# Where in an expert's group the zero rows for a later group are sent: behind the results of the group ahead, or in the middle of the group

## The chip, the cores and the metric

The kernel runs on one core of a Trainium2 chip. The metric is the device time of one execution in microseconds, the median of several runs. A core has TensorE (PE, matrix products), VectorE (DVE), ScalarE (ACT), GpSimd (POOL) and SyncE (SP); SP and POOL issue nearly all of the transfers here, SP by hardware queues and POOL by one software queue. A line such as L842 is line 842 of the kernel.

## The reference

Attention over 4 batches, 8 heads, 768 positions and 64 columns a head, with a mask that keeps the first `n_global` keys and the last `n_local`, and a bias by distance. Its output, 3072 tokens of 512 values, goes through a layer of 8 experts; each token uses only the expert with the highest gate.

```python
logits = x @ w_gate
expert_idx = np.argmax(logits, axis=1)
...
for e in range(E):
    mask = expert_idx == e
    ...
    xe = x[mask]
    h = np.maximum(xe @ w1[e], 0.0)
    ye = h @ w2[e]
    out[mask] = gate_w[mask, None] * ye
```

Here `w1[e]` is 512 x 1024 and `w2[e]` 1024 x 512, all in 32-bit floats.

## The kernel before

**Stages.** The first 160 us or so are attention, 24 blocks of 128 positions. Each block's tokens are sent by an indirect transfer (`scatter`, L627) to a table in HBM, `xg_dram`, which has one region of rows for each expert. Then come the groups, in the order 0, 8 (a small one, for late tokens of expert 0), 1, 2, ..., 7: one expert at a time, up to 512 token rows. With some 3072 / 8 = 384 tokens to an expert, the rows of a region behind the last token would hold whatever lay in HBM before, so rows of zeros are written there.

**The zeros.** For groups 0, 1 and 8 all 512 (or 128) rows are cleared beforehand by SP (`blank`). For groups 2 to 7, `pads(g)` issues four indirect transfers from POOL (L755), one for each 128 rows of the region, with the table `pad` of row numbers: a row that holds a token gets a number beyond the table, and the transfer leaves it out. The source is `zeros`, 128 rows of 516 words in SBUF.

**A group.** `group(p)` computes the up product (512 to 1024), ReLU, and the down product (1024 to 512). Both use a scheme with seven block products in place of eight (`seven`): the up product is made in two halves `j` of seven steps, the down product in one, so that a group has steps 0 to 13 and D = 14 to 20. A step of the up product is eight matmuls, one of the down product sixteen. The products are called one, two, three, four, five, six and last, in this order of issue. In each, TensorE writes a PSUM bank (L842), and a reader takes it: ScalarE copies product one (L870), VectorE takes two (L874), ScalarE three (L879, with ReLU, into the tile `h`; L881 in the down product), VectorE four (L885), five (L901), six (L906) and last (L911), each of the last three followed by a ReLU on ScalarE (L866). Product three adds to the bank of product one, so it waits for L870's copy. In the first half of groups 1 to 7, the columns beyond 208 of the first four products are made in a separate part ahead of product five, `rest` (L889 to L897). L879 of the second half (step 9) writes `h[:, 2:4, 0]`.

VectorE also makes the sums that the scheme needs: of the weights (`w_sums`, L710 to L713), of the tokens (`x_sums`, L812 to L815) and of the hidden values (`h_sums`, L925 to L928), and turns the tokens (`x_in`, L806).

**Order of the other work.** Engines run the instructions in the order in which the program records them. `at_(i, ...)` hangs work behind step i. In group p, with `nxt` the next group and `after` the one behind that:

- at the start SP loads the next group's tokens and gates, which wait for that group's zeros: `ex.load_x(nxt, [f"pad{nxt}.{j}" for j in range(4)])` (L779 and L788);
- in steps 0 and 1 the results of the group ahead are turned back (L821), scaled with the gate (L824) and sent to the output by four indirect transfers from POOL (`send`, L832);
- behind step 4 POOL issues `pads(after)`. Nothing on POOL lies between the sends and these;
- behind D and D + 6 SP loads the weights of `after` (L690, L693).

`pads(2)` is issued ahead of these, in group 0, by `all_counts`; groups 1 to 5 issue `pads(3)` to `pads(7)`.

**Waits.** The program records what each operation reads and writes (`_r` and `_w` add to it) and derives from that which semaphores it waits for. A transfer's reads and writes count until it has landed.

Of the kernel before, what the change touches and what calls it, by code (L numbers as in the profile page):

```python
# [634 lines left out]
class Experts:  # L635
# [113 lines left out]
            out=self.xs[g * self.REGION:g * self.REGION + 128 * n, :].rearrange("(j p) w -> p j w", p=128),  # L749
            in_=self.zero.bitcast(I32).unsqueeze(1).to_broadcast([128, n, self.XW]), _w=[f"pad{g}"], _r=[self.zero])  # L750

    def pads(self, g):

        for j in range(4):
            self.f.pool.indirect_dma_start(  # L755
                out=self.xs[:], out_offset=bass.IndirectOffsetOnAxis(ap=self.keep["pad"][:, g, j:j + 1], axis=0),
                in_=self.zeros.bitcast(I32), in_offset=None, bounds_check=self.xs.shape[0] - 1, oob_is_err=False,
                _r=[self.keep["pad"][:, g, j:j + 1], self.zeros], _w=[f"pad{g}.{j}"])

    def pad_table(self, g0, g1):  # L760
        k, V = self.keep, self.f.dve
# [214 lines left out]
def kernel(  # L976
# [60 lines left out]
    with ExitStack() as stack:  # L1037
# [6 lines left out]
        f = Flow(tc)  # L1044
# [3 lines left out]
        ex = Experts(f, dict(moe_w1=moe_w1, moe_w2=moe_w2, xs=xg_dram, XW=XW, REGION=NTOK, out=out), psum, keep,  # L1048
                     (Arena(big, 0, WSET), Arena(big, WSET, WSET)), Arena(big, 2 * WSET, 22560 - 2 * DM), small[:, 0:XW], ylast[:])
# [26 lines left out]
        def sums_part(n):  # L1076

            us = at.sums(n - 2, U)
            at.tokens_x(n - 2, T0)
            us()  # L1080
            at.tokens_u(n - 2, U)
# [109 lines left out]
        def all_counts():  # L1191
            V.tensor_tensor(keep["cnt"][:, 1:E], base_e[:, 1:E], keep["gbase"][:, 1:E], ALU.subtract)
            ex.tables(1, E)
            ex.pad_table(2, E)
            f.pool.memset(ex.zeros, 0.0)
            ex.pads(2)

        order = [0, E, *range(1, E)]
        forms = [(keep["index"][0:1, g:g + 1], ex.SIZES, f"form{g}") for g in range(E)]
# [39 lines left out]
        def group(p):  # L1239

            g = order[p]
            nxt = order[p + 1] if p + 1 < len(order) else None
            after = order[p + 2] if p + 2 < len(order) else None
            todo = {}

            def at_(i, *fns):
                todo.setdefault(i, []).extend(fns)

            def run(steps, first):
                for i, fn in enumerate(steps, first):  # L1250
                    fn()
                    for fn in todo.pop(i, ()):
                        fn()
# [35 lines left out]
            if g == 0:  # L1289

                run(ups[:1], 0)
                sums_part(N + 1)
                run(ups[1:2], 1)
                pieces = ex.w_pieces(1)

                def scatters():
                    for u in range(NBLK):
                        at.scatter(B - 1, u)
                    last = sum(tokens, [])
                    ex.load_x(E, last)  # L1300
                    for fn in pieces[:4]:
                        fn()
                    ex.load_x(1, last)

                at_(2, lambda: at.normal(N - 1, U), lambda: at.choose(B - 1), *pieces[4:])
                at_(4, lambda: at.counts(U), lambda: at.gates(B - 1))
                at_(5, lambda: at.slots(B - 1, U))
                at_(6, lambda: at.rows(N - 1, T0), scatters)
                at_(9, late_counts)
                at_(D, all_counts)  # L1310
                at_(D + 3, lambda: ex.marks(E))
                at_(D + 4, lambda: ex.x_in(E, 0))
            elif g == E:
                sums, pieces, xs = ex.w_sums(1, True), ex.w_pieces(2), ex.x_sums()
                at_(0, sums[0], sums[1])
                at_(1, sums[2], check_sums)
                at_(2, check)
                at_(3, lambda: f.hint(*forms[1]), lambda: ex.x_in(1, 0), lambda: ex.x_in(1, 1), xs[0], xs[1])
                at_(4, xs[2], xs[3], lambda: ex.marks(1), *pieces[:4])
                at_(5, *pieces[4:])  # L1320
            else:
                if nxt is not None:
                    sums, xs = ex.w_sums(nxt, True), ex.x_sums()
                    at_(13, lambda: ex.x_in(nxt, 0))
                    at_(D + 1, lambda: ex.x_in(nxt, 1), sums[0])
                    at_(D + 3, xs[0], xs[1])
                    at_(D + 4, sums[1])
                    at_(D + 5, sums[2])
                    at_(D + 6, xs[2], xs[3], lambda: ex.marks(nxt))
                if after is not None:  # L1330
                    pieces = ex.w_pieces(after)
                    at_(4, lambda: ex.pads(after))
                    at_(D, *pieces[:4])
                    at_(D + 6, *pieces[4:])

# [9 lines left out]
        for p in range(len(order)):  # L1345
            group(p)
# [429 lines left out]
```

## Time and profile before

| | us |
|---|---|
| median of 3 runs | 517.89 (516.78 to 520.77) |
| the profiled execution's own time | 517.95 |
| its span, first to last instruction | 516.1 |
| TensorE busy | 478.7 |
| VectorE busy | 352.5 |
| ScalarE busy | 174.1 |
| GpSimd busy | 166.0 |

The profile is of one execution. A row of the table by stage has the stretch in us from the start, its length, then for PE, PEld (weight loads), DVE, ACT and POOL the busy time and the number of instructions, then TensorE's granted clock, the mean busy share of the 16 DMA engines, and GB/s. A row of the waits has who waited, for whom, the sum in us, how often, and the longest. A row of the timeline has start and length in us, engine, line, operation, what it writes and reads, and in brackets how long the engine was idle before and what ended that. An end of a matmul is modelled, and some matmul records can be missing. A transfer of POOL is shown for the time in which POOL works on it.

### The profile page before, as it was taken

What the parts mean: (1) busy time and instruction counts of PE and PEld (TensorE: products, weight loads), DVE (VectorE), ACT (ScalarE), POOL (GpSimd) and SP (SyncE); (2) the same over time, 40 slices, a digit from 0 to 9 for tenths busy, and PEclk for the clock granted to TensorE, in tenths of its full rate; (3) what the DMA queues carried; (4) which work ended last, traced back from release to release, by engine and by line L of the source; (5) the groups of instructions that cost most, each with busy time, mean ns of one, the idle gap of its engine ahead of it and who ended that gap; (6) DMA issues with size and microseconds to landing.
All of it is one profiled execution on the core that took longest, in us unless ns stands there. A gap on an engine that the chain in (4) does not pass through costs nothing. (4 is left out here: it accounts for less than half of the span.)

```text
span 516.1 us, 10775 instructions
## 1 busy us (share of the span) xinstructions
PE 478.7 (93%) x4397; PEld 451.3 (87%) x4397; DVE 352.5 (68%) x626; ACT 174.1 (34%) x306; POOL 166.0 (32%) x192
## 2 busy tenths in 40 slices
PE   3999999999977999999998999997999999999980
PEld 3888888888866899999998999997999999999980
DVE  4654775897873884666775885865877667687840
ACT  3766555555543230323122223212204203303410
POOL 1554465667664053330024016006006103003011
PEclk9999999999997999999999999999999999999996
DMA  9999999998424437897783774656368378001000
GB/s 152 205 242 244 183 238 245 241 224 187 103 99 110 161 127 165 210 244 175 162 222 116 159 211 117 144 186 164 75 176 219 101 181 228 7 1 48 18 25 29
DMA packets 120344, 79.24 MB, mean 154 GB/s; under 512 B 86422, under 2 KB 103318, under 8 KB 120272
## 3 DMA queue, kind: packets, MB, share of 16 engines
q1 hardware_dynamic: 112960, 63.77, 55.9%
q0 software_dynamic: 6480, 14.45, 8.0%
q8 instruction: 51, 0.84, 0.7%
q14 instruction: 21, 0.17, 0.1%
q10 hardware_dynamic: 832, 0.02, 0.1%
HBM read 61.39 MB, written 23.71 MB: 165 GB/s over the span
## 5 line engine op out<-in xcount | busy, mean ns | idle before, releaser
L842 PE MATMUL psum<-arena 128*128 128x208 f32 (+5 forms) x1776 | 293.4, 325 | 8.1 <-ACT arena L870 6.5
L842 PEld LDWEIGHTS psum<-arena 128*128 128x128 f32 x1776 | 285.1, 190 | 12.6 <-ACT arena L870 8.0
L832 POOL DMA_INDIRECT out_dram<-arena,to x16 | 21.8, 1365 | 218.5 <-ACT arena L824 193.8
L501 DVE TENSOR_TENSOR arena<-psum,arena 128x1024 f32<-128x1024 f32 x40 | 48.8, 1219 | 37.2 <-PE psum L491 37.2
L515 POOL TENSOR_TENSOR arena<-arena 128x512 f32<-128x512 f32 x40 | 53.4, 1334 | 35.9 <-ACT arena L509 35.9
L509 ACT ACTIVATE arena<-arena 128x1024 f32<-128x1024 f32 (+1 forms) x48 | 47.4, 987 | 47.7 <-DVE arena L501 36.1
L491 PE MATMUL psum<-arena 64*128 64x128 f32 x704 | 50.2, 291 | 1.2 <-ACT arena L477 0.7
L866 ACT ACTIVATE arena<-arena 128x512 f32<-128x512 f32 x48 | 30.2, 630 | 61.2 <-DVE arena L901 30.8
L491 PEld LDWEIGHTS psum<-arena 64*128 64x128 f32 x704 | 45.0, 197 | 5.9 <-issue 3.4
L528 PE MATMUL psum<-arena 128*64 128x128 f32 x704 | 43.9, 277 | 0.2 <-issue 0.2
L870 ACT COPY arena<-psum 128x512 f32<-128x512 f32 (+1 forms) x24 | 13.5, 561 | 84.8 <-PE psum L842 83.2
L528 PEld LDWEIGHTS psum<-arena 128*64 128x64 f32 x704 | 38.2, 137 | 3.3 <-issue 0.6
L627 POOL DMA_INDIRECT xg_dram<-arena,slot_i x24 | 24.7, 1030 | 23.3 <-DVE arena L911 15.8
L911 DVE TENSOR_TENSOR arena<-arena,psum 128x512 f32<-128x512 f32 x24 | 16.5, 689 | 21.9 <-PE psum L842 18.3
L885 DVE TENSOR_TENSOR arena<-arena,psum 128x512 f32<-128x512 f32 (+1 forms) x24 | 15.8, 659 | 22.0 <-PE psum L842 20.7
L755 POOL DMA_INDIRECT xg_dram<-small,pad x24 | 25.7, 1070 | 12.5 <-issue 7.0
L906 DVE TENSOR_TENSOR arena<-arena,psum 128x512 f32<-128x512 f32 x24 | 16.5, 688 | 15.9 <-PE psum L842 14.2
L901 DVE TENSOR_TENSOR arena<-arena,psum 128x512 f32<-128x512 f32 x24 | 16.5, 688 | 14.8 <-PE psum L842 13.6
L467 PE MATMUL psum<-ident,arena 128*128 128x128 f32 x96 | 16.1, 294 | 8.7 <-DMA arena<-in_k_dram 7.1
L832 POOL DMA_INDIRECT out_dram<-ylast,to x17 | 17.4, 1025 | 20.6 <-ACT ylast L824 12.7
L874 DVE TENSOR_TENSOR arena<-arena,psum 128x512 f32<-128x512 f32 (+1 forms) x24 | 15.8, 656 | 11.0 <-PE psum L842 9.8
L713 DVE TENSOR_TENSOR arena<-arena 128x1024 f32<-128x1024 f32 x16 | 19.9, 1243 | 3.0 <-issue 2.9
(152 smaller groups left out, 535.2 us busy)
## 6 DMA issues: line engine op xcount, KB each, us to landing
arena<-in_moe_w_dram SPq DMA_DIRECT2D x64, 512.0 KB
arena<-xg_dram SPq DMA_DIRECT2D x64, 128.0 KB
arena<-in_q_dram SPq DMA_DIRECT2D x24, 256.0 KB
arena<-in_k_dram SPq DMA_DIRECT2D x24, 256.0 KB
arena<-in_v_dram SPq DMA_DIRECT2D x24, 256.0 KB
xg_dram<-arena SPq DMA_DIRECT2D x2, 1032.0 KB
xg_dram<-arena,slot_i POOLq DMA_INDIRECT x24
xg_dram<-small,pad POOLq DMA_INDIRECT x24
```

What stands on the lines that cost most here:

```text
L491: f.pe.matmul(self.psum[:, 2 * g + a, c:c + P], lhsT=kt[r, m, :], rhs=qt[r, m, :], start=True, stop=True, skip_group_check=True)
L501: f.dve.tensor_tensor(e, s, self.bias[:, g, :, 1:3, :].rearrange("p h k c -> p h (k c)"), ALU.add)
L509: f.act.activation(e, e, AF.Exp)
L515: f.pool.tensor_tensor(self.es[n % 3][:, g], e[:, :, 0:P], e[:, :, P:2 * P], ALU.add)
L528: f.pe.matmul(po[r, m, :], lhsT=self.v[(n - ab) % 6][:, 2 * m + a, :], rhs=self.e[n % 2][:, m // 2, 2 * a + m % 2, P * ab:P * ab + P], sta ...
L627: self.f.pool.indirect_dma_start(out=self.xs[:], out_offset=bass.IndirectOffsetOnAxis(ap=k["slot_i"][:, b % 2, u:u + 1], axis=0), in_=self ...
L713: lambda: V.tensor_tensor(c["t4"], c["b21"], c["t2"], ALU.subtract)]
L755: self.f.pool.indirect_dma_start(out=self.xs[:], out_offset=bass.IndirectOffsetOnAxis(ap=self.keep["pad"][:, g, j:j + 1], axis=0), in_=sel ...
L832: return pool.indirect_dma_start(out=self.out[:], out_offset=bass.IndirectOffsetOnAxis(ap=self.keep["to"][:, g, j:j + 1], axis=0), in_=sel ...
L842: f.pe.matmul(self.psum[:, bank, 256 * t + cut.start:256 * t + cut.stop], lhsT=w[k][:, ts(t, 128)], rhs=x[k][:, cut], start=(fresh and t = ...
L866: f.act.activation(d, d, act)
L901: V.tensor_tensor(dst["c22"], u3, bank(W), ALU.add)
```

## The change

`pads` gets a second argument, `behind`, which each of its four transfers is declared to read: nothing is taken from it, but the transfers wait until it has been written, and a later write to it waits until they have landed. In groups 1 to 5 the call moves from behind step 4 to behind step 10, with `h[:, 2:4, 0]` as that argument, which L879 writes in step 9. `pads(2)` stays where it is and names `zeros`, which it reads anyway. The same transfers are issued, in the same order on every engine.

```diff
-    def pads(self, g):
+    def pads(self, g, behind):
...
-                _r=[self.keep["pad"][:, g, j:j + 1], self.zeros], _w=[f"pad{g}.{j}"])
+                _r=[self.keep["pad"][:, g, j:j + 1], self.zeros, behind], _w=[f"pad{g}.{j}"])
...
-            ex.pads(2)
+            ex.pads(2, ex.zeros)
...
-                    at_(4, lambda: ex.pads(after))
+                    at_(10, lambda: ex.pads(after, ex.h[:, 2:4, 0]))
```

## The prediction

> **What bounds the kernel now**
>
> I read the page first, then the busy times by stage, TensorE's waits in the expert stage, and last the timeline around each run of GpSimd's transfers.
>
> ```profile
> PE 478.7 (93%) x4397; PEld 451.3 (87%) x4397; DVE 352.5 (68%) x626; ACT 174.1 (34%) x306; POOL 166.0 (32%) x192
> L755 POOL DMA_INDIRECT xg_dram<-small,pad x24 | 25.7, 1070 | 12.5 <-issue 7.0
> ```
>
> TensorE is the bound. GpSimd is idle for two thirds of the span, so time saved or lost on it counts only through what it disturbs. The stage table covers groups 1 to 6, one row each: length, then TensorE's busy time.
>
> ```profile
> 226.00:265.00 39.00, 39.00 (x224) 38.97 (x223) 26.48 (x37) 7.57 (x14) 5.13 (x5) 1.00 0.77 188
> 265.00:305.00 40.00, 37.72 (x243) 37.35 (x242) 29.84 (x43) 10.07 (x18) 8.43 (x8) 1.00 0.64 163
> 305.00:346.00 41.00, 40.44 (x243) 39.75 (x242) 29.68 (x42) 10.11 (x19) 10.25 (x8) 1.00 0.59 153
> 346.00:388.00 42.00, 38.47 (x247) 37.62 (x246) 30.00 (x43) 10.44 (x20) 8.75 (x8) 1.00 0.61 156
> 388.00:430.00 42.00, 41.81 (x244) 41.11 (x242) 29.75 (x43) 10.23 (x20) 10.18 (x8) 1.00 0.62 159
> 430.00:470.00 40.00, 39.56 (x235) 38.86 (x234) 28.73 (x40) 9.39 (x17) 4.85 (x4) 1.00 0.25 64
> ```
>
> TensorE loses 7.0 us here in all, nearly all in two groups. The clock column is 1.00 throughout, so no throttle is behind it. The waits from 225 to 470 us name what ended the idle time:
>
> ```profile
> PE psum L842 <- ACT arena L870: 6.5, 4, 3.5
> PE psum L842 <- DVE arena L901: 0.4, 1, 0.4
> ```
>
> All four waits for L870 (ScalarE's copy of product one) fall at the same step, the start of the second half of the up product: 2.28 us at 279.6, 0.52 at 318.2, 3.51 at 362.1 and 0.19 at 400.7. The worst, in the timeline:
>
> ```profile
> 352.81 5.79 PE L842 MATMUL psum<-arena 128*128 128x184 f32 x35
> ...
> 354.03 0.97 POOL L755 DMA_INDIRECT xg_dram<-small,pad  x1 [0.30 <-issue]
> ...
> 356.64 0.69 DVE L906 TENSOR_TENSOR arena<-arena,psum 128x512 f32<-128x512 f32 x1 [2.11 <-PE psum L842]
> ...
> 357.87 0.97 POOL L755 DMA_INDIRECT xg_dram<-small,pad  x1 [0.30 <-issue]
> 360.22 0.69 DVE L911 TENSOR_TENSOR arena<-arena,psum 128x512 f32<-128x512 f32 x1 [2.89 <-remote]
> ...
> 361.48 0.57 ACT L870 COPY arena<-psum 128x512 f32<-128x512 f32 x1
> ...
> 362.10 25.04 PEld L842 LDWEIGHTS psum<-arena 128*128 128x128 f32 x160 [3.79 <-ACT arena L870]
> 362.10 25.36 PE L842 MATMUL psum<-arena 128*128 128x184 f32 x160 [3.51 <-ACT arena L870]
> ```
>
> TensorE's records run on without a gap to 358.6, eight matmuls in 1.25 us, but the engines that take its results get them late: L906 comes 2.80 us after L901, L911 3.58 us after L906. So TensorE had computed and its signals were late; then it stops, because product three may not start before L870 has copied product one. GpSimd is meanwhile in the second half of an unbroken row of eight indirect transfers, four sends (L832) and four of zeros (L755), from 347.96 to 358.84.
>
> I then set each such row against TensorE's idle time. Rows of eight (from 267.2, 307.0, 348.0, 389.5): 2.28, 0.52, 3.51, 0.19 us. Five (one send, four of zeros, 227.3 to 233.7): none. Four sends alone (from 208.8, 431.3, 472.2): 0, 0.43, 0. Four of zeros alone (196.8 to 201.6): none. Six scatters from 182.9: none; but six from 147.6 end with the 2.7 us wait of L553. Signals are late from about 6 us after the row's start. Two rows without loss:
>
> ```profile
> 193.81 12.99 PE L842 MATMUL psum<-arena 128*128 128x176 f32 x86
> ...
> 438.70 7.54 PE L842 MATMUL psum<-arena 128*128 128x200 f32 x43 [0.43 <-DVE arena L901]
> ```
>
> The first spans the four transfers of zeros by themselves with TensorE never idle; the second shows the dearest row of sends alone.
>
> **What the Trainium skill says**
>
> "Perfetto Trace Analysis", section "Tensor Engine Instruction (MATMUL, LD_WEIGHTS)": a matmul's end in the profile is estimated, and the semaphore moves only after PSUM has acknowledged the writes. So unbroken matmul records beside late readers are possible, as seen here; why the signal comes late it doesn't say.
>
> The same page, "DMA Instruction — SWDGE (GPSIMD)": the interval shown ends when descriptors are written, not when data moves. The trace agrees: the last one of zeros ends at 358.84, and GpSimd's queue moves packets until after 360.
>
> "SBUF — State Buffer", section "Who interferes with whom": a VectorE operation with two SBUF inputs contends with GpSimd instructions that read SBUF, and the first one holds the port. Here one side pays: a transfer beside L712 takes 2.02 instead of 0.97 us, while L712 itself takes 1.22 to 1.28 us.
>
> "DMA: Bandwidth & Descriptors", section "SWDGE vs HWDGE vs iDMA": GpSimd's transfers have one queue, and the engines take turns between it and the hardware queues. So zeros today stand behind the sends in one queue. The page gives nothing on signals of TensorE.
>
> **The change part by part**
>
> Counts: no instruction goes. Five groups (1 to 5) issue pads four times each, so 20 transfers of 0.97 us, 1.28 us from start to start, move from step 4 to step 10. The first additionally waits for L879 of the second half. pads(2) keeps its place; its extra argument adds nothing.
>
> 1. *The row of eight is cut.* In the group from 305 the zeros now run from 313.5 to 319.4; L879 ends at 320.5, so they would run from about 320.6 to 325.4 (3 x 1.28 + 0.97), some 7 us behind the last send. The stalls of the four rows of eight go: -6.5 us. What is left is four rows of sends alone: by the three seen, 0.43 us in three, 0.14 each, so +0.6 us (0 to 1.7). Group 1 has only one send before its zeros and loses nothing today.
>
> 2. *The zeros in the new place.* They lie beside products four to seven of the second half and the start of the down product. Nearest row: the four alone at 196.8, no stall. But the place is tighter: in the group from 430 product five ends near 436.9 by TensorE's records and L901 starts at 437.95, a signal some 1.0 us late that cost 0.43 us, so it had about 0.5 us to spare; and the down product's second product needs L926, which ends at 327.6, about 0.4 us before TensorE comes to it. I take 0, and keep 0.5 us for each of five groups (2.5 us) as the upper end. Below zero it can't go: TensorE has no gap there to win.
>
> 3. *VectorE.* Beside the zeros it has L925 to L928, nine sums with two SBUF inputs, instead of L712. At most 0.06 us each (1.28 against 1.22), 0.5 us a group, inside the same 0.4 to 0.5 us of room, and inside the upper end above. Taken as 0.
>
> 4. *The added waits.* GpSimd's wait holds only the other three pads; behind them come the next group's sends, some 20 us later. L879 now also waits for the four transfers of the group before, since they count as readers of that tile; these landed over 30 us earlier, and L879 stands idle 1.6 us for TensorE today. 0, at most 0.2 us on ScalarE, which is 34% busy.
>
> 5. *Who reads the zeros, and the other queues.* load_x of the next group waits for them in SP's queue, at 345.3 for the zeros that would land near 328: 17 us of room. The weight loads at 325.6 may share the engines with 0.26 MB of zeros for about 1.5 us at the 179 to 229 GB/s seen there; those weights are read one group later. 0.
>
> Sum: -6.5 + 0.6 = -5.9 us on the profiled execution's 517.95 us: 512.05, say 512.1. Its own time lies 0.06 us from the median 517.89, so nothing is added. Ends: 511.4 (no residue) and 511.4 + 1.7 + 2.5 = 515.6.
>
> **The rivals**
>
> *The lateness goes along with the zeros* (B). For it: late signals lie beside the zeros rather than the sends in all four rows, and in the row from 348 they go on after other transfers have ended. Against it: zeros alone at 196.8 and one send with zeros at 227.3 cost nothing. Then about 6 us come back in the new place: 517.9, between 515.6 and 519.
>
> *It was never the row* (C). The small loads of gates (8 bytes each) and the instruction fetch near 354.3 fall in the same microseconds, and stay. For it: the group from 430 has such loads and a fetch, no zeros, and a late signal; against it: that cost 0.43 us, not 3.5. 517.9.
>
> *Slower* (D). Zeros are late on their own and strike where there is only 0.4 to 0.5 us of room, in five groups instead of four. Priced by the two worst stalls, mean 2.9 us, with 0.4 us less room: 3.3 x 5 - 5.9 = +10.6 us, 528.5. It decides against the change from 1.2 us of new idle time a group (5.9 / 5), and over 1% from 2.2 us. Against it: again the row at 196.8.
>
> **How the numbers follow**
>
> The likeliest case 0.66, B 0.16, C 0.07, D 0.11. A measurement of this kernel tells about 1% from no change (5.2 us). The likeliest case passes that if the residue stays below 1.3 us, three times in four: faster 0.50. Within 1%: 0.16 of it and B and C, 0.39. Slower: D, 0.11. The likeliest case by itself spans 511.4 to 515.6; the range reaches a little below it for the scatter of the runs (516.78 to 520.77) and up to 518.2 to take in most of B and C; D is left out.
>
> **What would show it**
>
> Right: TensorE's waits for L870 fall from 6.5 us to under 1.5; L901, L906 and L911 follow each other at one product's length (1.25 to 1.41 us) again; GpSimd's rows in groups 2 to 5 break into four and four, with L755 about 0.1 us behind L879. Wrong: waits for L901, L874 or L885 of the down product in their place (B, D), or L870 still waited for beside rows of four (C).

## The result, and the profile after

The kernel after takes 509.94 us (509.14 to 512.12, 5 runs) against 517.89 us (516.26 to 520.77): ratio 0.986, 95% interval 0.9824 to 0.9896, faster by 1.4%. The forecast, 512.1 us, had the direction and the mechanism; the gain was 7.95 us where 5.9 was worked out, and the time lies 1.1 us below the range. The profiled execution after is the fastest of its five (509.14 us).

The page after, engines and the group of the zeros:

```profile
PE 476.9 (94%) x4397; PEld 452.2 (89%) x4397; DVE 352.8 (70%) x626; ACT 174.0 (34%) x306; POOL 163.4 (32%) x192
L755 POOL DMA_INDIRECT xg_dram<-small,pad x24 | 23.4, 974 | 52.5 <-ACT arena L879 41.5
```

The same 24 transfers, now behind a wait for L879 (41.5 us of idle time on GpSimd) and each a little shorter, 974 ns in place of 1070: in the kernel before, three of them that began while L711 or L712 was running had taken 1.23, 2.02 and 1.94 us, and none begins there now. Next the table by stage, cut at the first L870 of each group so that each row is one whole group, 1 to 6:

```profile
225.12:264.95 39.83, 39.83 (x230) 39.79 (x229) 26.64 (x37) 8.24 (x16) 4.88 (x5) 1.00 0.77 189
264.95:302.24 37.29, 37.29 (x242) 37.21 (x241) 29.61 (x42) 9.96 (x18) 8.42 (x8) 1.00 0.65 173
302.24:342.10 39.86, 39.86 (x242) 39.79 (x241) 29.64 (x42) 10.09 (x18) 9.20 (x8) 1.00 0.62 157
342.10:379.69 37.59, 37.57 (x242) 37.18 (x241) 29.62 (x42) 9.97 (x19) 8.75 (x8) 1.00 0.66 170
379.69:420.82 41.13, 41.13 (x242) 41.06 (x241) 29.62 (x42) 10.07 (x18) 9.20 (x8) 1.00 0.67 160
420.82:460.97 40.15, 40.13 (x242) 39.74 (x241) 29.63 (x42) 10.09 (x19) 4.84 (x4) 1.00 0.28 71
sum 235.85, PE 235.82 PEld 234.78 DVE 174.75 ACT 58.42 POOL 45.29; mean PE 39.30 PEld 39.13 DVE 29.13 ACT 9.74 POOL 7.55
```

TensorE is busy for 235.82 of 235.85 us. The same cut of the kernel before, its groups 2 and 4, which had lost most, and the sum of all six:

```profile
265.17:305.01 39.84, 37.56 (x242) 37.19 (x241) 29.68 (x42) 10.07 (x18) 8.43 (x8) 1.00 0.64 163
345.97:387.50 41.53, 38.00 (x242) 37.15 (x241) 29.53 (x42) 9.97 (x19) 8.75 (x8) 1.00 0.60 154
sum 244.84, PE 237.84 PEld 234.50 DVE 174.67 ACT 58.47 POOL 47.60; mean PE 39.64 PEld 39.08 DVE 29.11 ACT 9.75 POOL 7.93
```

The span fell by 8.8 us (516.1 to 507.3): 8.99 in these six groups and 0.22 ahead of group 1, while 0.41 came back behind group 6. By group, 1 to 6, the fall is 0, 2.55, 1.10, 3.94, 0.72 and 0.68 us. The weight loads' time is the same to 0.3 us: no work went, only idle time. TensorE's waits from 225 to 470 us by its weight loads, in the kernel before:

```profile
PEld psum L842 <- ACT arena L870: 7.7, 4, 3.8
PEld psum L842 <- DVE arena L874: 1.3, 4, 0.3
PEld psum L842 <- DVE arena L901: 0.7, 1, 0.7
```

and what is left of them after:

```profile
PEld psum L842 <- DVE arena L874: 0.7, 2, 0.3
PEld psum L842 <- DVE arena L901: 0.2, 1, 0.2
```

No wait for L870 remains. In the timeline, the group that had lost most:

```profile
347.81 10.49 PE L842 MATMUL psum<-arena 128*128 128x208 f32 x66
...
349.68 0.69 DVE L901 TENSOR_TENSOR arena<-arena,psum 128x512 f32<-128x512 f32 x1 [0.19 <-issue]
...
350.85 0.69 DVE L906 TENSOR_TENSOR arena<-arena,psum 128x512 f32<-128x512 f32 x1 [0.49 <-PE psum L842]
...
352.10 0.69 DVE L911 TENSOR_TENSOR arena<-arena,psum 128x512 f32<-128x512 f32 x1 [0.56 <-PE psum L842]
...
353.36 0.57 ACT L870 COPY arena<-psum 128x512 f32<-128x512 f32 x1
...
357.31 0.97 POOL L755 DMA_INDIRECT xg_dram<-small,pad  x1 [7.45 <-ACT arena L879]
```

L901, L906, L911 and L870 follow each other every 1.17 to 1.26 us, one product's length, where they had been 2.80, 3.58 and 1.26 us apart; GpSimd rests 7.45 us between the last send and the first zeros.

The traces also hold the times at which each engine's semaphore was raised, the signal that the readers wait for. In group 4 of the kernel before, three products end by TensorE's records at 356.10, 357.35 and 358.59 us; matched in order (a few are missing from the trace), their signals come at 360.20, 360.29 and 360.38 us, so 4.10, 2.94 and 1.79 us late, where half of all of TensorE's signals follow within 0.02 us. Three products that take 1.25 us each were not computed in 0.18 us, so it was the signals that were late and not the work. No signal of VectorE, ScalarE or GpSimd is over 0.02 us late in that trace. In the kernel after, none of TensorE's that the trace holds is over 0.3 us late in groups 1 to 6.

### The profile page after: what moved, and what is told of

Read it like the earlier page. It is cut to its first block, busy times and chain, and to the rows that moved or that the text cites. A ratio compares the mean times of both kernels' runs of the same rounds, so it can differ in the third digit from the quotient of the medians.

```text
span 507.3 us, 10785 instructions
## 1 busy us (share of the span) xinstructions
PE 476.9 (94%) x4397; PEld 452.2 (89%) x4397; DVE 352.8 (70%) x626; ACT 174.0 (34%) x306; POOL 163.4 (32%) x192
## 5 line engine op out<-in xcount | busy, mean ns | idle before, releaser
L870 ACT COPY arena<-psum 128x512 f32<-128x512 f32 (+1 forms) x24 | 13.5, 561 | 81.8 <-PE psum L842 81.6
L755 POOL DMA_INDIRECT xg_dram<-small,pad x24 | 23.4, 974 | 52.5 <-ACT arena L879 41.5
L911 DVE TENSOR_TENSOR arena<-arena,psum 128x512 f32<-128x512 f32 x24 | 16.5, 688 | 17.7 <-PE psum L842 17.2
L906 DVE TENSOR_TENSOR arena<-arena,psum 128x512 f32<-128x512 f32 x24 | 16.5, 688 | 14.7 <-PE psum L842 13.4
L901 DVE TENSOR_TENSOR arena<-arena,psum 128x512 f32<-128x512 f32 x24 | 16.5, 688 | 12.8 <-PE psum L842 11.5
L874 DVE TENSOR_TENSOR arena<-arena,psum 128x512 f32<-128x512 f32 (+1 forms) x24 | 15.8, 657 | 8.5 <-PE psum L842 8.1
```

The lines of the kernel that those rows point to most:

```text
L755: self.f.pool.indirect_dma_start(out=self.xs[:], out_offset=bass.IndirectOffsetOnAxis(ap=self.keep["pad"][:, g, j:j + 1], axis=0), in_=sel ...
L901: V.tensor_tensor(dst["c22"], u3, bank(W), ALU.add)
```

## The experiments

Each kernel was timed beside the kernel before on the same chip, on three chips in all. The kernel before took 513.11 us beside four of them (the place without the wait, all rows written, gates loaded later, eight zeros in the middle), 514.29 us beside the next four (the kernel after once more, the first split, the short pause, the row of six cut at the end of attention) and 518.03 us beside the last four (the second split, rows of nine and twelve, the late place, memsets). Ratios with their intervals are therefore what is compared, and the length of each group in the profiled execution, cut as above. The table gives how much longer each group was than in the kernel after (differences of -0.01 are given as 0.00). Each row is one execution; the kernel before was profiled only in the first measurement, on another chip than these three:

| kernel | group 1 | 2 | 3 | 4 | 5 | 6 |
|---|---|---|---|---|---|---|
| before | 0.00 | 2.55 | 1.10 | 3.94 | 0.72 | 0.68 |
| after, once more | 0.00 | 0.01 | 0.00 | 0.00 | 0.01 | 0.77 |
| place without the wait | 0.00 | 3.84 | 0.00 | 1.78 | 0.01 | 0.00 |
| all rows written | 0.00 | 1.77 | 0.00 | 1.45 | 0.00 | 0.00 |
| gates loaded later | 0.00 | 1.78 | 0.00 | 1.39 | 0.01 | 0.00 |
| split, left-out rows behind the sends | 0.00 | 1.11 | 0.00 | 1.03 | 0.01 | 0.00 |
| split, written rows behind the sends | 0.00 | 0.19 | 0.00 | 1.13 | 0.48 | 0.00 |
| rows of nine and twelve | 1.16 | 0.01 | 2.15 | 0.00 | 0.43 | 0.00 |
| eight zeros in the middle | 0.00 | 0.00 | 0.41 | 0.00 | 0.21 | 0.00 |
| short pause | 0.00 | 0.01 | 0.00 | 0.01 | 0.34 | -0.19 |
| late place | 0.00 | 0.01 | 0.60 | 0.00 | 0.01 | 0.08 |
| memsets | 0.00 | 0.01 | 0.00 | 0.11 | 0.01 | 0.67 |
| scatters of four and two | 0.00 | 0.01 | 0.00 | 0.00 | 0.01 | 0.00 |

One thing in this table goes against a simple rule. Groups 2 to 5 all have a row of eight in the kernel before and in the three kernels that keep all four zeros behind the sends (place without the wait, all rows written, gates loaded later). Groups 2 and 4 lost 1.4 to 3.9 us each time; groups 3 and 5 lost 1.10 and 0.72 us in the kernel before and nothing in the other three, where no signal beside that row is over 0.25 us late. So the length of a row alone does not settle what it costs. Groups 2 and 4 are the shorter ones (37.29 and 37.59 us after, against 39.86 and 41.13); whether that is why they suffer, no run tests.

**The kernel after, once more**

> The kernel after, unchanged, on the same chip as the three others. It was 0.986 of before on another chip; here before itself stands idle less (513.1 us median in the batch before), so with the rows of eight gone, 508 to 510 us, 0.990 to 0.994, with a smaller scatter than before's. No wait of TensorE for L870.

508.48 us (507.76 to 508.82), ratio 0.9886 (0.9814 to 0.9959). The gain holds in a second set of runs; the ratio is a little below the 0.990 to 0.994 expected. The 0.77 us in group 6, four sends alone with a late L901, are there in this execution and not in the first one: this is a residue of the sends, which comes and goes.

**The place without the wait**

```diff
-                    at_(10, lambda: ex.pads(after, ex.h[:, 2:4, 0]))
+                    at_(10, lambda: ex.pads(after, ex.zeros))
```

> The kernel after, with the call behind step 10 but with zeros in place of h as the tile that it names, so that nothing on GpSimd waits. If the wait is what does the work, GpSimd sends the zeros straight behind the sends again, the rows of eight are back, TensorE waits 5 to 8 us for L870 and the time is that of before, 516 to 520 us. If the place in the program's order matters, it stays near 510 us.

514.2 us, ratio 1.0014 (0.9987 to 1.0041): no difference from before. The place in the program's order did nothing here; GpSimd sends the zeros as soon as it may. The wait is what moves them.

**All rows written**

```diff
-        V.scalar_tensor_tensor(inv, inv, float(2 ** 22), sl, ALU.mult, ALU.add)
+        V.scalar_tensor_tensor(inv, inv, 1024.0, sl, ALU.mult, ALU.add)
```

> The kernel before, but a row of the zeros' table that holds a token gets row + 1024 in the same region, which nothing reads, in place of a number beyond the table: all 128 rows of each transfer are written, 2064 bytes each, and there are no packets of 8 bytes for rows left out. If these small packets make the signals late, TensorE's waits for L870 fall from 6.5 us to under 2 us and the time to 510 to 513 us. If the row of eight does it by the number of transfers, the waits stay at 5 to 8 us: 516 to 520 us, or a little more for the 4 MB that are written in addition.

514.3 us, ratio 1.0019 (0.9994 to 1.0045). The stalls stay in groups 2 and 4 (1.77 and 1.45 us); the profiled execution is the fastest of the 20. The packets of left-out rows are not the cause.

**Gates loaded later**

```diff
...
-                    ex.load_x(nxt, [f"pad{nxt}.{j}" for j in range(4)])
+                    ready = [f"pad{nxt}.{j}" for j in range(4)]
+                    ex.load_x(nxt, ready, gates=False)
+                    at_(12, lambda: ex.load_gates(nxt, ready))
```

> The kernel before, but SP loads the next group's gates (L788, 8 bytes a row) behind step 12 and not at the group's start, so that they no longer lie beside the sends and the zeros. If the gates' small packets are what makes the signals late or adds to it, TensorE's waits for L870 fall under 3 us and the wait for L901 in group 6 goes: 510 to 514 us. If the row of eight does it alone, the waits stay at 5 to 8 us: 516 to 520 us.

512.71 us, ratio 0.9996 (0.9971 to 1.0021). The lines left out (`...`) make a function `load_gates` of the gates' part of `load_x`. TensorE waited 1.5 us for the copy of product one (line 878 in this kernel), and 0.7 us more at the same step in group 4; this was the fastest of the 20 executions. The waits are under the 3 us that would have spoken for the gates, but the two groups lost as much as with all rows written, on the same chip (1.78 and 1.39 us against 1.77 and 1.45), and the ratio of 20 runs shows no gain. Rival C's gates are out. Its instruction fetch was not moved by itself, but it stays where it was in the kernel after (8.4 us into group 4, 8.3 before), which doesn't stall.

**The two splits**

```diff
-                    at_(10, lambda: ex.pads(after, ex.h[:, 2:4, 0]))
+                    at_(4, lambda: ex.pads(after, ex.zeros, (0, 1)))
+                    at_(10, lambda: ex.pads(after, ex.h[:, 2:4, 0], (2, 3)))
```

> The zeros split: the two transfers of rows 0 to 255, which hold tokens and so are left out row by row, directly behind the sends (a row of six), the two of rows 256 to 511 in the middle. If the length of the row decides, with lateness only from about the sixth transfer on, TensorE waits for L870 under 1 us in all: 508 to 511 us, close to the kernel after. If the left-out rows' packets of 8 bytes decide, waits of several us remain: 512 us or more, close to before.

The new last argument of `pads` says which of the four transfers it issues. 509.69 us, ratio 0.9898 (0.9872 to 0.9925).

```profile
PE psum L842 <- ACT arena L870: 1.5, 2, 0.8
```

Two waits of 0.7 to 0.8 us, 1.5 us in all where under 1 was expected: in these groups, 2 and 4, less than rows of eight and more than rows of four. The other split has (2, 3) at step 4 and (0, 1) at step 10:

> The other split: the two transfers of rows 256 to 511, of which most are really written, directly behind the sends (a row of six), the two of left-out rows in the middle. If the number of transfers in a row decides, this behaves as the first split did: two waits for L870 of about 0.7 us, 509 to 511 us, ratio about 0.990. If the data that the zeros move counts, more remains than there: 511 to 513 us.

511.47 us, ratio 0.9882 (0.9858 to 0.9905), the groups 1.8 us longer in all than after's, against 2.1 in the first split. With the written rows or the left-out ones behind the sends, the loss is much the same in sum, one execution each on two chips, though it falls in part on other groups. Together with all rows written, this speaks for the number of transfers and against the bytes that they move.

**Rows of nine and twelve, and of four, at the old place**

```diff
-                    at_(4, lambda: ex.pads(after))
+                    if after != 4 and after != 6:
+                        at_(4, *[lambda g=g: ex.pads(g) for g in range(after, min(after + 2, E))])
```

> The kernel before, but groups 1 and 3 send the zeros of two groups directly behind the sends (rows of nine and of twelve transfers), group 5 those of one (eight), groups 2 and 4 none (four sends alone); nothing more or less is sent in all. If lateness grows with the length of the row at this place, group 3 stands idle longer than any row of eight did (over 3 us), group 1 gets a stall, and groups 2 and 4 stand idle under 0.5 us each; the total may come out like before's, 511 to 517 us. If the stalls belong to the groups and not to the rows, groups 2 and 4 keep theirs.

513.76 us, ratio 0.9941 (0.9911 to 0.9971). Groups 1 to 5 in the table by stage:

```profile
226.14:267.13 40.99, 40.35 (x230) 39.68 (x229) 26.62 (x37) 8.23 (x15) 10.05 (x9) 1.00 0.76 189
267.13:304.43 37.30, 37.30 (x242) 37.22 (x241) 29.62 (x42) 9.97 (x18) 4.52 (x4) 1.00 0.65 164
304.43:346.44 42.01, 40.66 (x242) 39.67 (x241) 29.63 (x42) 10.08 (x19) 14.08 (x12) 1.00 0.61 157
346.44:384.02 37.58, 37.57 (x242) 37.17 (x241) 29.62 (x42) 9.98 (x19) 4.85 (x4) 1.00 0.64 162
384.02:425.58 41.56, 41.40 (x242) 41.01 (x241) 29.62 (x42) 10.08 (x18) 10.11 (x8) 1.00 0.63 159
```

The count of GpSimd's instructions (x9, x4, x12, x4, x8) is the row's length, and the idle time moves with it: group 1, which lost nothing with a row of five, loses 1.16 us with nine; groups 2 and 4, which lost most in the kernel before, are down to after's lengths with four. This is the clearest of the runs: same place, same transfers in all, and the loss moves with the rows. That group 3 would lose over 3 us was too much; twelve cost 2.15.

**Eight zeros in the middle**

```diff
-                    at_(10, lambda: ex.pads(after, ex.h[:, 2:4, 0]))
+                    if after != 4 and after != 6:
+                        at_(10, *[lambda g=g: ex.pads(g, ex.h[:, 2:4, 0]) for g in range(after, min(after + 2, E))])
```

> The kernel after, but groups 1 and 3 send the zeros of two groups, eight transfers in a row, in the middle, and groups 2 and 4 none; nothing more or less is sent in all. If the length of a row of indirect transfers is what makes TensorE's signals late (row theory), the middle of groups 1 and 3 shows VectorE late for L901, L906 or L911 of the second half and TensorE idle there or at the start of the down product, 0.5 to 3.5 us each: 511 to 516 us. If it takes sends and zeros together, or the gates' loads (8 bytes each) beside them, no new idle time: 509 to 511 us.

508.76 us, ratio 0.9916 (0.9883 to 0.9949); the groups together are 0.6 us longer than after's. The end of the row of eight in group 3:

```profile
315.76 15.46 PE L842 MATMUL psum<-arena 128*128 128x200 f32 x88
...
325.40 0.97 POOL L755 DMA_INDIRECT xg_dram<-small,pad  x1 [0.30 <-issue]
327.84 0.69 DVE L874 TENSOR_TENSOR arena<-arena,psum 128x512 f32<-128x512 f32 x1 [2.50 <-remote]
```

The signal is late here as well (VectorE idle 2.50 us ahead of L874 while TensorE's matmuls run on to 331), as the row theory says, and it needs no sends ahead of it. But the cost that I had expected, 0.5 us at least, was not there: 0.41 us in group 3, none in group 1. The products of the down stage take sixteen matmuls, which may be what leaves room; that was not tried apart. So a long row makes a signal late in the middle too, and there it costs less.

**A short pause, and a late place**

```diff
-                    at_(10, lambda: ex.pads(after, ex.h[:, 2:4, 0]))
+                    at_(6, lambda: ex.pads(after, ex.h[:, 4:6, 0]))
```

> The four zeros behind step 6 of the first half, waiting for L866 behind product last, so that they start 2 to 4 us behind the last send, not 7. If a pause of this length lets the late signals catch up (length of the unbroken row), no wait for L870: 508 to 511 us. If it is the number of transfers within some 12 us, or the place at the start of the second half, where product three waits for L870's copy, the waits stay: 512 to 515 us.

508.2 us, ratio 0.9886 (0.9814 to 0.9959), the same as after beside it. GpSimd rested 4.53 us in group 2 and 4.08 in group 3, and the zeros began at the start of the second half, just where the stalls had been. So it is not the place; a pause of 4 us was enough. A shorter one wasn't tried.

```diff
-                    at_(10, lambda: ex.pads(after, ex.h[:, 2:4, 0]))
+                    at_(D + 2, lambda: ex.pads(after, ex.yt[:, 0:2, 0]))
```

> The four zeros behind step D + 2, waiting for L881 of the down product, so that they lie some 20 us behind the sends and 8 to 10 us ahead of the next ones. If only the cut of the row counts, it is as good as the kernel after: 508 to 509.5 us, no wait for L870. If the middle of the group is what matters (a place with room for late signals), waits appear in the down product (L874, L881) or at the next group's start: 510 us or more.

510.44 us, ratio 0.9873 (0.9787 to 0.9959). The time is above the 508 to 509.5 us expected, on the chip where the kernel before was slowest; the ratio is again as good as after's (0.986 and 0.9886), and there is no wait for L870. The 0.60 us in group 3 lie beside the sends.

**Memsets in the place of the transfers**

```diff
+                    at_(4, *[lambda: f.pool.memset(ex.zeros, 0.0) for _ in range(8)])
                     at_(10, lambda: ex.pads(after, ex.h[:, 2:4, 0]))
```

> The kernel after, with eight memsets of the tile zeros (about 0.5 us each on GpSimd) directly behind the sends, where the zeros' transfers stood before, so that GpSimd is busy without a break for some 10 us; the transfers stay in the middle. If it is GpSimd's unbroken work that makes the signals late, the waits for L870 come back: 511 to 515 us. If it is transfers, nothing changes: 508 to 509.5 us.

509.61 us, ratio 0.9867 (0.9784 to 0.9951). GpSimd's own timeline in group 2:

```profile
271.80 0.98 POOL L832 DMA_INDIRECT out_dram<-ylast,to  x1 [0.30 <-issue]
272.76 4.66 POOL L1332 MEMSET small<- 128x516 f32 x8
280.33 0.97 POOL L755 DMA_INDIRECT xg_dram<-small,pad  x1 [2.91 <-ACT arena L879]
```

But for 0.3 us between sends GpSimd is busy from the first send to 277.4, and groups 1 to 5 lose 0.12 us in all. The 0.67 us in group 6, where there are no memsets, are the sends' residue again. GpSimd being busy is not the cause; indirect transfers are.

**The row of six at the end of attention**

```diff
-            for _ in range(NBLK if b == B - 1 and i >= 3 else 1):
+            for _ in range(4 if b == B - 1 and i >= 3 else 1):
...
-            if n == N - 3:
+            if n == N - 2:
                 ex.load_x(0, sum(tokens[:B - 1], []))
```

> The kernel after, with the row of six scatters of the third batch at the end of attention (147 to 155 us) cut into four and two: two go with the next block, and the load of group 0's tokens moves one block back, behind them. Before and after both show TensorE idle 2.7 us at 157 us for L545, whose input's signal was late. If a row of six makes that, this wait falls under 0.5 us: 2 to 2.7 us less than the kernel after, 506 to 508 us. If that signal is late for another reason, the wait stays; if the tokens of group 0 then come too late for L806 near 168 us, TensorE stands idle there instead.

512.57 us, ratio 0.9964 (0.9942 to 0.9986): 4 us more than after. TensorE's waits from 140 to 180 us:

```profile
PE psum L842 <- DVE arena L806: 4.1, 1, 4.1
PE psum L553 <- ACT arena L545: 2.2, 2, 1.8
```

The wait for L545 fell from 2.7 us to 1.8, not under 0.5. By the semaphore's times, signals are still up to 2.98 us late beside the four scatters, against 4.54 beside the six in the kernel after. Why four cost so much there stays open. And group 0's tokens came 4.1 us late for L806. This attempt to beat the kernel after failed.

## Why the prediction was right, and where it was wrong

*The view of the bound*: right. It is TensorE's idle time at one step of the groups, and that is what went.

*Step 1, the row of eight is cut*: the mechanism is right and is shown: with rows of eight back (place without the wait) the stalls of groups 2 and 4 are back; at the old place in these two groups, rows of four lose nothing, rows of six 0.2 to 1.1 us and rows of eight 1.4 to 3.9. In groups 1 and 3, rows of nine and twelve lose 1.2 and 2.2 us. **This is also the step that failed: its two terms were mis-sized.** The stalls were priced at 6.5 us, the sum of the PE row's waits for L870. But that row's matmuls overlap, and each is drawn longer (0.32 us) than the distance to the next (0.156 us in the group from 346), so a gap on it begins late. The weight loads of the same group show 3.79 us where the PE row shows 3.51. Over groups 1 to 6, PE idle is 244.84 - 237.84 = 7.0 us and PEld idle 244.84 - 234.50 = 10.3; after, PEld idle is 1.1. The difference, 9.3, is close to what the groups gave (8.99). The prediction's own table had the weight loads in the column beside the one that was read. By the waits of the weight loads, those for L870 fell by 7.7 us, where 6.5 had been counted; those for L874 fell by 0.6, which the sum did not have, since the PE row does not show them; and 0.2 us without a named cause went. The Trainium skill ("Perfetto Trace Analysis", section "Identifying the Most-Contended Engine") says that TensorE's matmul busy time is not a good measure of how close a kernel is to its limit, since pipelined instructions look smaller in the trace, and to use the busy share of the weight loads, beside the share of peak arithmetic, instead. This case agrees, for idle time too: 9.3 us by the weight loads, 7.0 by matmuls, 8.99 measured.

The other term, +0.6 us of residue from sends alone, was 0 in this execution, and it took group 6's loss as something that stays. There the wait for L901 fell by 0.5 us and the group by 0.68; 0.77 came back in the second execution of the same kernel. The residue shows in group 6 of three of the fourteen profiled executions; that it was absent here is chance. Together the two terms should have read -9.0 for this execution in place of -5.9: with the 0.2 us that came back at the ends, 517.95 comes to 509.1, the time of the profiled execution after. The medians lie 7.95 us apart.

*Step 2, the new place*: 0 was right for four zeros. The upper end, 0.5 us a group, was not reached even by eight in that place (0.41).

*Steps 3 to 5*: right as far as the runs show. VectorE's busy time is 352.5 and 352.8 us; no wait for landed zeros, weights or L879's added semaphores shows on TensorE. Two small misses: L755 starts 0.8 us behind L879's end (356.52 to 357.31), not 0.1; and the sums of step 3 are eight a group in the traces, not nine, of which only one begins beside the zeros of group 4 (L925 at 361.43, zeros from 357.31 to 362.1).

*The rivals*: B (lateness goes along with the zeros) fell: four in the middle, late in the group, or after a short pause cost nothing. C fell with the gates; the fetch is still there after. D fell with the result, and with the eight in the middle. One argument used against B and D was weaker than it looked: beside the four zeros alone at 196.8, TensorE loses nothing, but two of its signals are 0.72 and 0.62 us late there (1.38 and 0.55 in the kernel after). So signals can be late without a cost.

What stays open is why a row of indirect transfers makes TensorE's signals late, and why the same row costs more in groups 2 and 4. The runs exclude GpSimd being busy as such, left-out rows, bytes moved and the gates; they show that the number in an unbroken row counts, with a cost beyond the residue of the sends from six on at the old place, and that 4 us of pause end it. No run looks inside the way that a signal takes.

## What to carry to other kernels

Where an engine's results are read late while its own records run on without a gap, look at what transfers are issued beside it, and count them in a row; a wait put on the queue that has time to spare can be cheaper than the row. Price idle time of TensorE from the weight loads' row or from the length of a whole stage, not from gaps between matmuls. A later place in the program's order moved nothing on an engine that was idle anyway (ratio 1.0014); only the wait did.

## What was unexpected of the hardware

Beside an unbroken row of indirect transfers on GpSimd, TensorE's signals came late, not its work: by up to 4.1 us in the groups of the kernel before. At the old place a row of eight cost 1.4 to 3.9 us in groups 2 and 4 and 0 to 1.1 us in groups 3 and 5, nine cost 1.2 (group 1) and twelve 2.2 (group 3); sends with eight memsets behind them cost at most 0.11 in groups 1 to 5. The size changed from run to run: 18 runs of the place without the wait spread over 510.98 to 518.34 us, 16 and 17 runs of the two splits only over 507.96 to 511.49 and 510.03 to 512.71.
